# Attention over four batches with two expert layers: values loaded in four parts, and three other pieces of the order moved

## The chip, the cores and the metric

The kernel runs on one core of a Trainium2 chip. The metric is the device time of one execution in microseconds (us). The engines are TensorE (PE; its weight loads are PEld), VectorE (DVE), ScalarE (ACT), GpSimd (POOL) and SyncE (SP), which issues nearly all transfers. L286 is line 286 of the kernel before.

## The reference

Attention with 4 batches, 12 heads, 448 positions and head size 64 mixes the scores over the heads before the softmax (`w_pre`) and the weights after it (`w_post`). Its output, 1792 rows of 768, goes through a layer with a squared ReLU, and then through a layer in which each row goes to one of 8 experts.

```
scores = scale * q @ k.T                              # per batch and head, 448 x 448
scores = einsum('bhij,hg->bgij', scores, w_pre)       # mix the heads
attn   = softmax(scores)
attn   = einsum('bhij,hg->bgij', attn, w_post)        # mix them again
x      = attn @ v                                     # -> 1792 x 768
x      = relu(x @ w_in)**2 @ w_out                    # first layer, d_ff 2048
out    = gate * (relu(x @ w1[e]) @ w2[e]), e = argmax(x @ w_gate)
```

## The kernel before

The order of the instructions on every engine is that in which the code is written; the framework adds the waits and moves nothing.

**Attention** runs in steps. A batch has 45 chunks of 10 query rows by 12 heads (120 partitions); step g belongs to chunk g of all 180, and o = 45 b is the first step of batch b. In step g, `norm` prepares chunk g+1 (sum, reciprocal, and `kp`, the mixing weights `kpost` divided by the sum), `pre` mixes the heads of chunk g+2 on TensorE, takes the maximum on VectorE and the exponential on ScalarE, and `post` multiplies chunk g by its `kp` on TensorE and copies the result out of PSUM into `at`. What else belongs to a step is entered with `on(step, function, ...)`: `scores` (q times k for a tile t of query rows and a head; ScalarE copies the product to `s`, a ring of four buffers, and SP sends it to its place in `t`), `prep` and `load` for the next batch, `pv` (TensorE multiplies `at` of nine chunks, a group `gr`, by the values `v`; half `hf` 0 has heads 0 to 5, half 1 has heads 6 to 11; ScalarE copies the product as `xh`), `pv_lo` (VectorE subtracts `xh` from the product, which gives `xl` and frees the PSUM bank) and `pv_out` (SP writes `xh` and `xl` to memory). A `pv` stands at the end of its step. There is one buffer `vt` for the values of a batch, 1.38 MB.

Before step 0 stands a stretch in which q and k of the first batch are transposed, split into a high and a low part (`zk`, `zl`, `zq`) and scored. There `prep` writes the high part of k twice, once into each half of the partitions; of the two second copies of a pair of heads ScalarE makes one (L211) and GpSimd the other (L209).

**The first layer** (`moe1`) begins inside attention: in the last batch `tail(rel)`, called at the end of step rel of it, runs a plan of weight loads and conversions (rel 27 to 47). In rel 42 to 45 the first products `up` run. The gate of the experts is folded into the weights of the layer: `gate_cols(w, acc, j)` makes two columns of w_out times w_gate on VectorE (L522), and `gate_parts` splits them (L529, L530). For the first two weight tiles, `late[0]` and `late[1]`, this is done late, by `late_gate(i, j)` with j from 0 to 3: the table `late_at` gives the step, and two calls stand in the first visit of `moe1`'s main loop (v = 0). j 0 and 1 need `wga`, j 2 and 3 need `wgb`, which are loaded in rel 39 and 41. The products of v = 0 (`down`, L719) are summed in PSUM banks that the last `pv` used. They do not need the gate's columns; those of v = 1 do.

The lines that the change touches decide on places alone:

```
if b == nb - 1 and c >= LATE:                       # L273, LATE = 32
    nc.scalar.mul(kp, kpost, mx[:, 3:4])
...
first, gap = (0, 1) if b == nb - 1 and gr == NGR - 1 else (1, 1) if b == nb - 1 else (1, 3)
...
if b > 0:
    on(o + 6, load_v, b)
...
late_at = {44: ((0, 0), (0, 1)), 45: ((0, 2), (0, 3)), 46: ((1, 0),), 47: ((1, 1),)}
```

Of the kernel before, what the change touches and what calls it, by code (L numbers as in the profile page):

```python
# [10 lines left out]
F32 = mybir.dt.float32  # L11
# [8 lines left out]
B, H, S, D = 4, 12, 448, 64  # L20
# [4 lines left out]
NP = H // 2  # L25
# [3 lines left out]
TOKT = 112  # L29
# [95 lines left out]
def attention(tc, cst, q, k, v, w_pre, w_post, xscr, nb, tail=None):  # L125
    nc = tc.nc
    GC = 9
    NGR = NCH // GC

    def left(name, bufs=1):  # L130
        return Areas(tc, name, bufs)

    wp, at1, vp, xp, mp = left("wp"), left("at1"), left("vp"), left("xp"), left("mp", 3)
# [10 lines left out]
    vt = {}  # L144
# [4 lines left out]
    halves = (slice(0, 64), slice(64, 128))  # L149

    XB = 4
    LATE = 32

    def load(b, p, nm):

# [20 lines left out]
    def prep(b, p, nm):  # L176

        z = zp.tile([128, 2, S], F32R, tag=f"z{nm}", name=f"z{nm}")
        x = xt.pop((b, p, nm))
        if b == 0:  # L180

            i = 2 * units.index((p, nm))
            pools = [(post_, pre_, post_, pre_, pv_)[j % 5] for j in (i, i + 1)]
            pys = [pool.tile([64, 4, 128], F32, name=pool.name) for pool in pools]
            for o in range(2):
                for r in range(4):
                    nc.tensor.transpose(pys[o][:, r, :TOKT], x[:, o, D * r:D * r + D], ident)
        else:
            py = qk.tile([128, 4, 128], F32, tag="qk", name="py")
            for r in range(4):  # L190
                nc.tensor.transpose(py[:, r, :TOKT], x[:, r].rearrange("p o d -> p (o d)"), ident)
            pys = [py[halves[o]] for o in range(2)]


        def rows(a, o=None):
            a = a if o is None else a[:, o]
            if nm == "k":
                return a.rearrange("q (r t) -> q r t", r=4)
            return a.rearrange("q (t r) -> q t r", r=4)

        yv = [y[:, :, :TOKT] for y in pys]
        if nm == "q":
            yv = [y.rearrange("q r t -> q t r") for y in yv]
        for o in range(2):
            nc.scalar.copy(rows(z[halves[o]], o), yv[o])
        if nm == "k":
            for o in range(2):
                if b == 0 and o and p < NP - 1:
                    nc.gpsimd.tensor_copy(z[halves[0], o], z[halves[1], o].bitcast(F32))  # L209
                elif b == 0:  # L210
                    nc.scalar.copy(rows(z[halves[1 - o]], o), yv[o])  # L211
        yield
        lo = None
        if nm == "k":
            fresh = len(zp.tags.get("zl", (0, ()))[1]) == 0 or zp.tags["zl"][0] < zp.bufs
            lo = zp.tile([128, 2, S], F32R, tag="zl", name="zl")
            if fresh:
                for o in range(2):
                    nc.gpsimd.memset(lo[halves[1 - o], o].bitcast(F32), 0.0)
        zt[b, p, nm] = (z, lo)  # L220
        for o in range(2):
            r = halves[o]
            dst = rows(z[halves[1 - o]], o) if nm == "q" else rows(lo[r], o)
            nc.vector.tensor_sub(dst, yv[o], rows(z[r], o).bitcast(F32))  # L224
            if nm == "k" and b > 0:
                nc.sync.dma_start(out=z[halves[1 - o], o].bitcast(F32), in_=z[r, o].bitcast(F32))
        yield

    def load_v(b):
        vt[b] = vp.tile([TOKT, H, 4, D], F32, name="v")  # L230
        for o in (0, H // 2):
            nc.sync.dma_start(
                out=vt[b][:, o:o + H // 2].rearrange("p h r d -> p h (r d)"),
                in_=v[b, o:o + H // 2].rearrange("h (p r) d -> p h (r d)", r=4),
            )

    tt = {}

# [29 lines left out]
    def norm(b, c):  # L268
        e, mx = st[b, c]
        nc.vector.tensor_scalar_add(mx[:, 2:3], mx[:, 1:2], 1e-9)  # L270
        nc.vector.reciprocal(mx[:, 3:4], mx[:, 2:3])  # L271
        kp = mp.tile([KP, KP], F32, tag="kp", name="kp")
        if b == nb - 1 and c >= LATE:  # L273
            nc.scalar.mul(kp, kpost, mx[:, 3:4])  # L274
        else:
            nc.gpsimd.tensor_scalar_mul(kp, kpost, mx[:, 3:4])  # L276
        st[b, c] = [e, kp]

    at = {}
# [91 lines left out]
    for i, w in enumerate((w_pre, w_post)):  # L371
        nc.sync.dma_start(
            out=wraw[:, i, :],
            in_=w.rearrange("(o h) g -> o h g", o=1).to_broadcast([II, H, H]),
# [14 lines left out]
    kpre, kpost = (wp.tile([KP, KP], F32, name=nm) for nm in ("kpre", "kpost"))  # L389
    mask = cst[:KP, C_MASK:C_MASK + II]  # L390
    for i, kf in enumerate((kpre, kpost)):
        nc.gpsimd.tensor_tensor(
            out=kf.rearrange("p (i g) -> p g i", i=II) if i == 0 else kf.rearrange("p (g i) -> p g i", i=II),
# [2 lines left out]
            op=ALU.mult,  # L396
        )
    nc.gpsimd.tensor_scalar_mul(kpre, kpre, 1.0 / float(D) ** 0.5)
    load_v(0)

    chunks = [(b, c) for b in range(nb) for c in range(NCH)]
    at_step = {}

    def on(g, f, *a):

        rank = 0 if f is go else 2 if f is begin else 1
        at_step.setdefault(g, []).append((rank, f, a))
# [10 lines left out]
    def spread(g, steps, f, *a):  # L418
        on(g, begin, (f, a), f, *a)
        for i in range(1, steps):  # L420
            on(g + i, go, (f, a))
# [5 lines left out]
    for b in range(nb):  # L427
        o = b * NCH
        for h in range(H):
            if b == 0:  # L430
                on(-4 + 8 * h // 12, scores, 0, 1, h)
            on(o + (4 if b == 0 else 2) + 10 * h // 12, scores, b, 2, h)
            on(o + 12 + 10 * h // 12, scores, b, 3, h)
            if b + 1 < nb:
                on(o + 26 + 11 * h // 12, scores, b + 1, 0, h)
                on(o + 37 + 10 * h // 12, scores, b + 1, 1, h)
        for gr in range(NGR):
            end = o + GC * gr + GC
            first, gap = (0, 1) if b == nb - 1 and gr == NGR - 1 else (1, 1) if b == nb - 1 else (1, 3)
            for hf in range(2):  # L440
                for i, f in enumerate((pv, pv_lo)):
                    on(end + first + gap * hf + i, f, b, gr, hf)
            on(end + first + gap + 2, pv_out, b, gr)
        if b + 1 < nb:
            for i, u in enumerate(units):
                spread(o + PREP[i], 2, prep, b + 1, *u)
                on(o + (PREP[i - XB] + 1 if i >= XB else 8 + i), load, b + 1, *u)
        if b > 0:
            on(o + 6, load_v, b)

    n = len(chunks)
    last = max(list(at_step) + [n])
# [28 lines left out]
def moe1(tc, cst, w_in, w_out, w_gate, xscr, tasks, st):  # L481
# [4 lines left out]
    nc = tc.nc  # L486
# [31 lines left out]
    def gate_cols(w, acc, i):  # L518

        dump = wr.tile([128, DM], F32, name="dump")  # L520
        for e in (2 * i, 2 * i + 1):
            nc.vector.scalar_tensor_tensor(  # L522
                out=dump, in0=w, scalar=1.0, in1=wg[e // 4][:, e % 4], op0=ALU.mult, op1=ALU.mult,
                accum_out=acc[:, e:e + 1],
            )
# [135 lines left out]
    }  # L661
    first = [up(0, 0, f) for f in range(GF)]
    UPS = {42: 0, 43: 0, 44: 1, 45: 1}
    late_at = {44: ((0, 0), (0, 1)), 45: ((0, 2), (0, 3)), 46: ((1, 0),), 47: ((1, 1),)}

    def late_gate(i, j):
        f, w, a = late[i]
        gate_cols(w, a, j)
        if j == 3:
            gate_parts(f, a)  # L670
# [86 lines left out]
    for v, (gi, b) in enumerate(order):  # L757

        def do(point):
            for f in tasks.get((v, point), ()):  # L760
                f()

        def conv(ago, stage, kinds="io"):
            i = piece.get(v - ago)
            if i is not None and pieces[i][1] in kinds:
                adv(i, stage)

        f0, f1 = gi * GF, gi * GF + 1
        conv(1, "hi")
        conv(0, "mask", "o")  # L770
        if 0 < v < len(order) - 1 and order[v + 1][1] != b:
            load_x(order[v + 1][1])
        if v > 0:
            for _ in up(gi, b, f0):
                pass
        do(1)
        conv(1, "lo")
        conv(0, "w0", "o")
        if v > 0:
            for i, _ in enumerate(up(gi, b, f1)):  # L780
                if i == 0:
                    do(2)
        conv(0, "w1", "o")
        conv(0, "mask", "i")
        if v in piece:
            load(piece[v] + 2)
        do(3)
        down(gi, b, f0, range(1))
        down(gi, b, f0, range(1, 3))
        do(4)  # L790
        if v == 0:
            late_gate(1, 2)
        down(gi, b, f1, range(1))
        do(5)
        down(gi, b, f1, range(1, 3))
        if v == 0:
            late_gate(1, 3)
        if v == 1:
            first_logits()
        do(6)  # L800
        if (gi, b) == (NG - 1, 2):
            close(y012, wgb, wga)
        do(7)
# [545 lines left out]
```

## Time and profile before

| | |
|---|---|
| median of 3 runs | 1351.9 us (1350.28 to 1353.49) |
| the profiled execution | 1351.87 us, span 1349.7 us |
| busy share of the span | PE 96%, PEld 85%, DVE 72%, ACT 56%, POOL 11% |
| mean granted clock of TensorE | 0.986 |
| attention and the first layer's start | 0 to about 552 us |

The span runs from the first to the last instruction of the profiled execution. The granted clock is 1.00 at 2.4 GHz and 0.50 at 1.2 GHz. Rows of the timeline begin with the start and the duration in us; a bracket at the end gives the idle time of the engine just before and what ended it.

### The profile page before, as it was taken

The numbers are of one execution on the slowest core, as the hardware profiler recorded it, in microseconds if no ns is written. First come the engines' busy times: TensorE is split into PE (matmuls) and PEld (weight loads), VectorE is DVE, ScalarE is ACT, GpSimd is POOL, SyncE is SP. The second block draws the span as 40 slices with busy tenths as digits, with TensorE's granted clock in tenths as the row PEclk, the third lists the DMA queues.
The fourth block names the chain that finished last, engine by engine and source line by source line (L and its number), as shares of the span: only waits on it lengthen the run. The fifth ranks groups of instructions, "written<-read, shape, count | busy, mean of one in ns | idle before, by whom it ended". The sixth has DMA issues, their size and how long they took to land. (4 is left out here: it accounts for less than half of the span.)

```text
span 1349.7 us, 24947 instructions
## 1 busy us (share of the span) xinstructions
PE 1291.3 (96%) x8875; PEld 1146.1 (85%) x8875; DVE 977.3 (72%) x1960; ACT 749.5 (56%) x1479; POOL 149.4 (11%) x229
## 2 busy tenths in 40 slices
PE   6999989998999898899999999999998999999997
PEld 4777867786787767899999999999997899999997
DVE  5567547665766357577895998689648588898887
ACT  6566546654655566353342433334234688889887
POOL 2222211221222110000000000000000111111101
PEclk9999989998999899899999999999999999999999
DMA  7666586548745458546373664636484594556551
GB/s 186 169 161 129 131 158 151 128 118 167 159 122 129 133 114 322 178 189 256 119 277 145 226 264 164 252 123 261 172 297 149 169 377 140 181 176 249 160 187 40
DMA packets 157638, 243.80 MB, mean 181 GB/s; under 512 B 84195, under 2 KB 128579, under 8 KB 149828
## 3 DMA queue, kind: packets, MB, share of 16 engines
q1 hardware_dynamic: 154708, 229.54, 55.3%
q0 software_dynamic: 2800, 12.61, 2.7%
q8 instruction: 72, 1.18, 0.4%
q14 instruction: 58, 0.48, 0.1%
HBM read 236.48 MB, written 23.21 MB: 192 GB/s over the span
## 5 line engine op out<-in xcount | busy, mean ns | idle before, releaser
L265 ACT ACTIVATE mp_e<-pre_pre,mp_mx 120x448 f32<-120x448 f32 x180 | 114.2, 635 | 145.0 <-DVE mp_mx L263 144.2
L286 PEld LDWEIGHTS post_post<-mp_kp,mp_e 120*112 120x112 f32 x1440 | 170.5, 176 | 23.5 <-ACT mp_kp L274 9.0
L286 PE MATMUL post_post<-mp_kp,mp_e 120*112 120x120 f32 x1440 | 178.6, 267 | 3.4 <-ACT mp_kp L274 3.2
L263 DVE TENSOR_REDUCE mp_mx<-pre_pre 120x1 f32<-120x448 f32 x180 | 110.0, 611 | 91.1 <-PE pre_pre L261 90.5
L627 PE MATMUL hp_h<-m1x_xl,m1w_ih 128*128 128x384 f32 (+1 forms) x480 | 155.7, 324 | 2.5 <-DMA m1x_xl<-xscrl 2.4
L636 ACT ACTIVATE m1g_r<-hp_h 128x384 f32<-128x384 f32 (+1 forms) x80 | 37.7, 471 | 214.9 <-PE hp_h L627 204.8
L627 PE MATMUL hp_h<-m1x_xh,m1w_ih 128*128 128x384 f32 (+1 forms) x480 | 156.1, 325 | 0.1
L627 PE MATMUL hp_h<-m1x_xh,m1w_il 128*128 128x384 f32 (+1 forms) x480 | 155.4, 324 | 0.0
L1102 DVE TENSOR_TENSOR m2w_w2l<-m2r_r,m2w_w2h 128x768 fp32r<-128x768 f32 x130 | 116.3, 953 | 33.8 <-ACT m2w_w2h L1101 33.7
L276 POOL TENSOR_SCALAR mp_kp<-wp_kpost,mp_mx 120x120 f32<-120x120 f32 x167 | 97.5, 584 | 371.1 <-DVE mp_mx L271 185.2
L245 PE MATMUL qk_qk<-zp_zk,zp_zq 128*120 128x448 f32 (+1 forms) x192 | 121.0, 630 | 5.9 <-DVE zp_zq L224 1.8
L294 DVE COPY at_at<-post_post 112x480 f32<-112x480 f32 x130 | 85.3, 657 | 50.6 <-PE post_post L286 50.1
L249 ACT COPY sp_s<-qk_qk 120x448 f32<-120x448 f32 (+1 forms) x188 | 96.0, 525 | 38.1 <-DMA tb_t<-sp_s 15.3
L719 PE MATMUL acc_a<-m1w_oh,m1g_gl 128*128 128x384 f32 (+1 forms) x436 | 113.1, 341 | 3.4 <-DVE m1g_gl L639 3.4
L719 PE MATMUL acc_a<-m1w_ol,m1g_gh 128*128 128x384 f32 (+1 forms) x436 | 112.3, 339 | 0.0
L719 PE MATMUL acc_a<-m1w_oh,m1g_gh 128*128 128x384 f32 (+1 forms) x436 | 112.1, 338 | 0.0
L733 DVE TENSOR_TENSOR y_y<-acc_a,y_y 128x384 f32<-128x384 f32 x196 | 96.4, 554 | 11.0 <-PE acc_a L719 10.7
L307 PE MATMUL pv_pv<-at_at,vp_v 112*64 112x90 f32 x1872 | 86.5, 252 | 13.8 <-DMA vp_v<-in_v 12.8
L1101 ACT CAST m2w_w2h<-m2r_r 128x768 fp32r<-128x768 f32 x130 | 99.1, 841 | 0.3 <-PE m2p_a L1163 0.2
L639 DVE TENSOR_TENSOR m1g_gl<-m1g_r,m1g_gh 128x384 fp32r<-128x384 f32 (+1 forms) x78 | 41.2, 528 | 77.7 <-ACT m1g_gh L638 77.7
L307 PEld LDWEIGHTS pv_pv<-at_at,vp_v 112*64 112x64 f32 x1872 | 79.3, 144 | 18.9 <-DMA vp_v<-in_v 13.4
L627 PEld LDWEIGHTS hp_h<-m1x_xl,m1w_ih 128*128 128x128 f32 x480 | 90.1, 188 | 3.3 <-DMA m1x_xl<-xscrl 3.3
(239 smaller groups left out, 2740.4 us busy)
## 6 DMA issues: line engine op xcount, KB each, us to landing
m2r_r<-in_moe_w SPq DMA_DIRECT2D x107, 512.0 KB
m2r_r<-in_moe_w SPq DMA_DIRECT2D x136, 384.0 KB
m1x_xh<-xscrh SPq DMA_DIRECT2D x29, 1152.0 KB
m1x_xl<-xscrl SPq DMA_DIRECT2D x29, 1152.0 KB
m1raw_rawi<-in_moe_w_in SPq DMA_DIRECT2D x16, 768.0 KB
m1raw_rawo<-in_moe_w_out SPq DMA_DIRECT2D x16, 768.0 KB
tb_t<-sp_s SPq DMA_DIRECT2D x48, 210.0 KB
ta_t<-sp_s SPq DMA_DIRECT2D x48, 210.0 KB
```

Of the source, the lines that this page charges most:

```text
L245: nc.tensor.matmul(pq[:m, :S], zq[:, n0:n0 + m], zkh, start=True, stop=False)
L249: eng(s[:m], pq[:m, :S])
L263: nc.vector.tensor_reduce(out=mx[:, 0:1], in_=pm[:KP, :S], axis=AX.X, op=ALU.max, negate=True)
L265: nc.scalar.activation(out=e, in_=pm[:KP, :S], func=AF.Exp, bias=mx[:, 0:1], accum_out=mx[:, 1:2])
L276: nc.gpsimd.tensor_scalar_mul(kp, kpost, mx[:, 3:4])
L286: nc.tensor.matmul(po[:, r].rearrange("p g i -> p (g i)"), ev[:, r], kp, start=True, stop=True)
L307: nc.tensor.matmul(px[64 * o:64 * o + 64, p], vt[b][:, g, r], a[:, r, g].rearrange("p c i -> p (c i)"), start=(r == 0), stop=(r == 3),)
L627: nc.tensor.matmul(ph, w[:, k], x, start=(kt == 0 and i == 0), stop=(kt == KT - 1 and i == 2))
L719: nc.tensor.matmul(p, g[:, c], w[:, HM * h:HM * h + (m if h else HM)], start=(j == 0 and i == 0), stop=(j == GF - 1 and i == 2),)
L733: nc.vector.tensor_add(y, p, y)
L1101: nc.scalar.copy(wh, raw)
L1102: nc.vector.tensor_sub(wl, raw, wh.bitcast(F32))
```

## The change

- `load_v` loads three heads at a time instead of six, so four parts instead of two, at steps o+3, o+5, o+7 and o+9 instead of both at o+6. For the first batch the parts stand at steps 1, 3, 5 and 7 instead of ahead of all steps.
- `pv` of the first four groups of batches 0 to 2 stands at the second and fourth step after its group's end instead of the first and fourth; that of their last group at the first and second instead of the first and fourth, so `pv_out` of it comes two steps earlier. The last batch keeps its places.
- GpSimd scales `kp` for the last 13 chunks too (before: ScalarE).
- In the stretch before step 0 GpSimd makes both second copies of k's high part for pairs 0 to 4 (before: one each).
- Of `late_gate`, (0, 1) goes from rel 44 to 45, (0, 2) and (0, 3) from 45 to 47, (1, 0) from 46 to 47, and (1, 1) from 47 to v = 0.

```
-                if b == 0 and o and p < NP - 1:
-                    nc.gpsimd.tensor_copy(z[halves[0], o], z[halves[1], o].bitcast(F32))
+                if b == 0 and p < NP - 1:
+                    nc.gpsimd.tensor_copy(z[halves[1 - o], o], z[halves[o], o].bitcast(F32))
...
-    def load_v(b):
-        vt[b] = vp.tile([TOKT, H, 4, D], F32, name="v")
-        for o in (0, H // 2):
-            nc.sync.dma_start(
-                out=vt[b][:, o:o + H // 2].rearrange("p h r d -> p h (r d)"),
-                in_=v[b, o:o + H // 2].rearrange("h (p r) d -> p h (r d)", r=4),
-            )
+    def load_v(b, i):
+
+        if i == 0:
+            vt[b] = vp.tile([TOKT, H, 4, D], F32, name="v")
+        o = slice(3 * i, 3 * i + 3)
+        nc.sync.dma_start(
+            out=vt[b][:, o].rearrange("p h r d -> p h (r d)"),
+            in_=v[b, o].rearrange("h (p r) d -> p h (r d)", r=4),
+        )
...
-        if b == nb - 1 and c >= LATE:
-            nc.scalar.mul(kp, kpost, mx[:, 3:4])
-        else:
-            nc.gpsimd.tensor_scalar_mul(kp, kpost, mx[:, 3:4])
+        nc.gpsimd.tensor_scalar_mul(kp, kpost, mx[:, 3:4])
...
-    load_v(0)
...
-            first, gap = (0, 1) if b == nb - 1 and gr == NGR - 1 else (1, 1) if b == nb - 1 else (1, 3)
+            first, gap = (2, 2) if gr < NGR - 1 and b < nb - 1 else (1, 1)
+            if b == nb - 1 and gr == NGR - 1:
+                first = 0
...
-        if b > 0:
-            on(o + 6, load_v, b)
+        for i in range(4):
+            on(o + 3 + 2 * i - 2 * (b == 0), load_v, b, i)
...
-    late_at = {44: ((0, 0), (0, 1)), 45: ((0, 2), (0, 3)), 46: ((1, 0),), 47: ((1, 1),)}
+    late_at = {44: ((0, 0),), 45: ((0, 1),), 47: ((0, 2), (0, 3), (1, 0))}
...
         if v == 0:
+            late_gate(1, 1)
             late_gate(1, 2)
```

On SP, at the start of the second batch, the order before was this (`tb_t` is where scores go, `vp_v` the values, `xscr` the output of `pv_out`, `ld_x` the next batch's q and k):

```order
L338 DMA xscrh_58<-xp_xh_663 768x1x64
L338 DMA xscrl_63<-xp_xl_664 768x1x64
L254 DMA tb_t_237<-sp_s_233 10x12x448
L232 DMA vp_v_404<-in_v 112x6x256 x2
L254 DMA tb_t_237<-sp_s_234 10x12x448
L254 DMA tb_t_237<-sp_s_235 10x12x448
L254 DMA tb_t_237<-sp_s_232 10x12x448
L166 DMA ld_x_593<-in_q 112x8x64
```

In the changed kernel the first part stands ahead of the output of `pv_out`, and a part follows after every three or four other transfers:

```order
L233 DMA vp_v_477<-in_v 112x3x256
L336 DMA xscrh_57<-xp_xh_681 768x1x9
L336 DMA xscrl_62<-xp_xl_682 768x1x9
...
L255 DMA tb_t_237<-sp_s_235 10x12x448
L255 DMA tb_t_237<-sp_s_232 10x12x448
L233 DMA vp_v_477<-in_v 112x3x256
L255 DMA tb_t_237<-sp_s_233 10x12x448
L255 DMA tb_t_237<-sp_s_234 10x12x448
L255 DMA tb_t_237<-sp_s_235 10x12x448
L233 DMA vp_v_477<-in_v 112x3x256
```

So the values no longer follow `pv_out` in one block.

On VectorE, at the end of attention, the order before was this (L639 is the low part of an `up` product, L522 the gate's columns, L323 is `pv_lo` of the last group, half 0 out of `pv_pv` and half 1 out of `pre_pre`):

```order
L639 TENSOR_TENSOR m1w_ol_4451<-m1g_r_4642,m1w_oh_4447 128x384
L522 SCALAR_TENSOR_TENSOR m1raw_dump_4661,m1raw_wog_4442<-m1raw_t_4387,wgb_wgb_4595 128x768 x4
L529 CAST m1w_oh_4444<-m1raw_wog_4442 128x8
L530 TENSOR_TENSOR m1w_ol_4448<-m1raw_wog_4442,m1w_oh_4444 128x8
L323 TENSOR_TENSOR xp_xl_664<-pv_pv_141,xp_xh_663 128x270
L522 SCALAR_TENSOR_TENSOR m1raw_dump_4661,m1raw_wog_4443<-m1raw_t_4333,wga_wga_4563 128x768 x2
L323 TENSOR_TENSOR xp_xl_664<-pre_pre_161,xp_xh_663 128x270
L522 SCALAR_TENSOR_TENSOR m1raw_dump_4661,m1raw_wog_4443<-m1raw_t_4333,wga_wga_4563 128x768 x2
```

In the changed kernel it is this, from the same operation on:

```order
L637 TENSOR_TENSOR m1w_ol_4459<-m1g_r_4650,m1w_oh_4455 128x384
L520 SCALAR_TENSOR_TENSOR m1raw_dump_4669,m1raw_wog_4450<-m1raw_t_4395,wga_wga_4571 128x768 x2
L321 TENSOR_TENSOR xp_xl_682<-pv_pv_141,xp_xh_681 128x270
L321 TENSOR_TENSOR xp_xl_682<-pre_pre_161,xp_xh_681 128x270
L520 SCALAR_TENSOR_TENSOR m1raw_dump_4669,m1raw_wog_4450<-m1raw_t_4395,wgb_wgb_4603 128x768 x4
L527 CAST m1w_oh_4452<-m1raw_wog_4450 128x8
L528 TENSOR_TENSOR m1w_ol_4456<-m1raw_wog_4450,m1w_oh_4452 128x8
L520 SCALAR_TENSOR_TENSOR m1raw_dump_4669,m1raw_wog_4451<-m1raw_t_4341,wga_wga_4571 128x768 x4
```

Two of the gate's operations stand between that L639 and the first `pv_lo` instead of four and their split, and none stands between the two `pv_lo`; all the others come behind them.

## Rows read from the trace of the kernel before

**Rows 1.** The waits of TensorE: us in total, times, longest.
```profile
PE pv_pv L307 <- DMA vp_v<-in_v: 12.8, 3, 4.7
PE acc_a L719 <- DVE xp_xl L323: 6.2, 2, 4.4
PE pre_pre L261 <- DMA ta_t<-sp_s: 5.8, 1, 5.8
...
PE post_post L286 <- ACT mp_kp L274: 3.2, 5, 1.2
```

**Rows 2.** The timeline of TensorE, `pv` of each later batch's first group.
```profile
188.31 3.87 PE L307 MATMUL pv_pv<-at_at,vp_v 112*64 112x90 f32 x48 [4.74 <-DMA vp_v<-in_v]
...
199.88 2.08 PE L307 MATMUL pv_pv<-at_at,vp_v 112*64 112x90 f32 x48
...
315.33 3.87 PE L307 MATMUL pv_pv<-at_at,vp_v 112*64 112x90 f32 x48 [4.03 <-DMA vp_v<-in_v]
...
442.04 3.87 PE L307 MATMUL pv_pv<-at_at,vp_v 112*64 112x90 f32 x48 [4.04 <-DMA vp_v<-in_v]
```

**Rows 3.** Stretches: us; busy of PE, PEld, DVE, ACT, POOL; clock; DMA share, GB/s.
```profile
35.00:40.00 5.00, 4.78 (x13) 2.69 (x12) 1.57 (x4) 1.44 (x4) 0.58 (x1) 0.73 0.75 200
...
190.00:195.00 5.00, 5.00 (x39) 3.82 (x36) 0.97 (x2) 1.11 (x3) 0.00 (x0) 0.53 0.80 189
...
320.00:325.00 5.00, 5.00 (x29) 3.73 (x27) 2.68 (x7) 2.76 (x9) 0.58 (x1) 0.90 0.79 192
...
445.00:450.00 5.00, 5.00 (x59) 3.89 (x58) 1.85 (x5) 1.96 (x5) 0.02 (x1) 0.77 0.37 123
...
545.00:550.00 5.00, 5.00 (x18) 5.00 (x18) 4.83 (x11) 0.00 (x0) 0.00 (x0) 0.53 0.89 158
```

**Rows 4.** The timeline of SP: the issues of the values, first and second batch.
```profile
28.23 1.19 SPq L232 DMA_DIRECT2D vp_v<-in_v  x2
...
179.85 2.52 SPq L232 DMA_DIRECT2D vp_v<-in_v  x2
```

**Rows 5.** The timeline of ScalarE: a copy of scores beside the values' transfer.
```profile
192.51 0.53 ACT L249 COPY sp_s<-qk_qk 120x448 f32<-120x448 f32 x1 [5.88 <-DMA tb_t<-sp_s]
```

**Rows 6.** DMA queues from 168 to 196 us: packets, MB, share of 16 engines.
```profile
q1 hardware_dynamic: 8809, 4.24, 81.3%
```

**Rows 7.** The timeline of TensorE: the first `pre`.
```profile
33.82 1.82 PE L261 MATMUL pre_pre<-tb_t,wp_kpre 120*120 120x448 f32 x2 [5.85 <-DMA ta_t<-sp_s]
```

**Rows 8.** The timeline of ScalarE: scores of head 9 (tile 0) and head 1 (tile 1).
```profile
25.16 0.52 ACT L249 COPY sp_s<-qk_qk 120x448 f32<-120x448 f32 x1
...
29.34 0.53 ACT L249 COPY sp_s<-qk_qk 120x448 f32<-120x448 f32 x1 [0.69 <-DMA tb_t<-sp_s]
```

**Rows 9.** The timeline of VectorE: scores of head 11, tile 0.
```profile
26.62 0.62 DVE L249 COPY sp_s<-qk_qk 120x448 f32<-120x448 f32 x1 [0.62 <-PE qk_qk L246]
```

**Rows 10.** The page's costliest groups: GpSimd's scaling (busy, mean ns, idle before it).
```profile
L276 POOL TENSOR_SCALAR mp_kp<-wp_kpost,mp_mx 120x120 f32<-120x120 f32 x167 | 97.5, 584 | 371.1 <-DVE mp_mx L271 185.2
```

**Rows 11.** The timeline of VectorE in the last steps: a reciprocal, a weight conversion.
```profile
501.65 0.16 DVE L271 RECIPROCAL mp_mx<-mp_mx 120x1 f32<-120x1 f32 x1
...
502.25 0.95 DVE L576 TENSOR_TENSOR m1w_il<-m1raw_t,m1w_ih 128x768 fp32r<-128x768 f32 x1
```

**Rows 12.** The timeline of TensorE: the first layer's first sums.
```profile
542.41 0.45 PE L719 MATMUL acc_a<-m1w_oh,m1w_oh 128*128 128x384 f32 x1 [4.38 <-DVE xp_xl L323]
544.64 0.69 PE L719 MATMUL acc_a<-m1w_oh,m1w_oh 128*128 128x384 f32 x1 [1.78 <-DVE xp_xl L323]
```

**Rows 13.** The timeline of VectorE around them.
```profile
536.43 0.56 DVE L639 TENSOR_TENSOR m1w_ol<-m1g_r,m1w_oh 128x384 fp32r<-128x384 f32 x1 [1.68 <-ACT m1w_oh L638]
537.63 0.96 DVE L522 SCALAR_TENSOR_TENSOR m1raw_dump<-m1raw_t,wgb_wgb 128x768 f32<-128x768 f32 x1 [0.64 <-DMA wgb_wgb<-in_moe_w_gate]
...
541.92 0.43 DVE L323 TENSOR_TENSOR xp_xl<-pv_pv,xp_xh 128x270 fp32r<-128x270 f32 x1
...
557.10 0.56 DVE L639 TENSOR_TENSOR m1g_gl<-m1g_r,m1g_gh 128x384 fp32r<-128x384 f32 x1 [6.24 <-ACT m1g_gh L638]
```

More of the change, by code (lines that the diff above doesn't have):

```diff
@@ L151, in attention @@
     XB = 4
-    LATE = 32
     def load(b, p, nm):
```

## The prediction

> **What bounds the kernel now.** I read the waits of TensorE first, since it is busy in 96% of the span, more than any other engine. The list is led by the places that the change touches: 12.8 us in three waits of `pv` for the values, 6.2 us in two waits of the first layer's sums for `pv_lo`, 5.8 us in one wait of the first `pre`, and 3.2 us in five waits of `post` for ScalarE's `kp` [rows 1]. Elsewhere in attention TensorE runs without a gap worth naming, so a wait taken away there shortens the span, unless another one takes its place.
>
> The timeline then shows that such a wait costs more than its idle time. In each of the batches 1 to 3 TensorE stands for 4.74, 4.03 and 4.04 us, and the 48 matmuls of the `pv` behind it take 3.87 us where those of a later half take 2.08 [rows 2]. The granted clock explains it: it has fallen to 0.50 (1.2 GHz) during the wait and comes back later. In 190 to 195 us its mean is 0.53, so it was low for 4.7 of these 5 us, to 194.7; in 320 to 325 the mean of 0.90 makes 1.0 us, to 321.0; in 445 to 450 the 0.77 makes 2.3 us, to 447.3 [rows 3]. Work at half clock loses half of its time: (194.7 − 188.31)/2 = 3.2, (321.0 − 315.33)/2 = 2.8 and (447.3 − 442.04)/2 = 2.6 us. The three waits cost 12.8 + 8.6 = 21.4 us.
>
> **Values in four parts (steps 3 to 9).** SP issues both halves at 179.85, and TensorE wants them at 188.31 − 4.74 = 183.57 [rows 2, 4]: 3.7 us for 1.38 MB, beside the output of `pv_out` that SP has just issued. Three steps lie between the two halves of `pv`, which start 11.57 us apart [rows 2]; less the clock's 3.2 us and 2 us for the first half itself, a step is about 2.1 us. In the changed kernel the first two parts leave 8 and 6 steps (17 and 13 us) ahead of the half that reads them, the last two 6 and 4 steps (13 and 8 us); in the last batch, whose `pv` keeps its places, the last part has two steps, some 4 to 5 us. Is there room? From 168 to 196 us the queue kept the 16 DMA engines busy for 81.3% [rows 6], 22.8 us of work, in a stretch that would last 28 − 4.74 − 3.2 = 20.1 us without the stall. So all of it would not fit, but the parts start about 6 us earlier, ahead of this burst. I take the three waits as gone.
>
> What remains is late scores: ScalarE waited up to 5.88 us for a buffer of the ring of four while the values travelled [rows 5], and it is in order, so the exponentials stand behind that. Bounds: nothing and 5.88 us per batch. The transfer that it waited for shared the engines with one block of 1.38 MB, and now with parts of 0.34 MB, so I take 1 us in each of the three batches. Term: 21.4 − 3.0 = **18.4 us**.
>
> **The first batch.** Its values were issued at 28.23, just behind the last scores of tile 0 [rows 4]. Head 9's scores, copied by 25.68, had left their buffer at 29.34, 3.66 us later [rows 8]. Head 11's, copied by 27.24 [rows 9], landed only as the first `pre` started, at 33.82 after 5.85 us of idle time [rows 7], if they are what it waited for: 6.6 us. Without the values beside them they should land at 27.24 + 3.66 = 30.9, which gives 2.9 us. The clock was low until 37.7 (mean 0.73 in 35 to 40 [rows 3]), so the low clock lost (37.7 − 33.82)/2 = 1.9 us; a wait shorter by half may still make it fall, so I take 0.9. The second copies: ScalarE loses five of about 0.52 us (the nearest row is a copy of 448 columns [rows 8]). 2.6 us is the upper bound and nothing the lower; VectorE works alongside with four subtractions and two thirds of a copy per pair, at the 0.62 of a copy [rows 9] 2.9 us against ScalarE's 3.3 before, so it takes over as the bound, and (3.3 − 2.9) × 5 = 2 us is left, of which I take half. Term: 2.9 + 0.9 + 1.0 = **4.8 us**.
>
> **GpSimd scales to the end.** The waits on ScalarE's `kp` are 3.2 us [rows 1], the most that this can give. But the operation lasts 0.584 us on GpSimd [rows 10], and between the weight conversions it is VectorE's reciprocal that comes late: in these steps VectorE goes from the reciprocal at 501.65 through the next maximum straight into a conversion at 502.25 [rows 11]. The rows of before give no step with a GpSimd scaling beside a conversion, so the bounds are a gain of 3.2 and a loss of 13 × 0.584 = 7.6 us, should each scaling hold up VectorE for its whole length. I take 0, between a shorter queue on ScalarE and a longer operation.
>
> The Trainium skill speaks against this edit ("SBUF — State Buffer", section "Who interferes with whom"): a VectorE instruction with two SBUF inputs and a GpSimd instruction that reads SBUF exclude each other for their whole length, and the one that issues first goes first. The conversion at 502.25 has two such inputs. No row of before shows the two at once; by the rule the edit would cost, in an estimate, 13 × (501.81 + 0.584 − 502.25) = 1.9 us, and the whole would come out at 1325.
>
> **The other moved `pv`.** The last group's halves of batches 0 to 2 now stand one step apart, so the second waits for `pv_lo` of the first. A step of 2.1 us holds the copy of `xh` and a subtraction of 0.43 us [rows 13]; the bounds are 0 and 0.5 us for each of the three, and I take **−0.5 us** in all.
>
> **The gate's preparations.** TensorE stands 4.38 and 1.78 us for the two `pv_lo` [rows 12]. VectorE reaches the first at 541.92, because after L639 (536.43 + 0.56 = 536.99) it waits 0.64 us for `wgb` and makes four gate operations and their split [rows 13]; 541.92 − 537.63 = 4.29 us for the four and the split makes some 1.0 us each. Now two stand there: `pv_lo` at 539.0, its bank free at 539.5, against the idle time's start at 542.41 − 4.38 = 538.03. So 1.5 us of the first wait stays, and the second goes, since the second `pv_lo` follows at once: 4.38 + 1.78 − 1.5 = 4.7. The low clock lasted until 549.7 (0.53 in 545 to 550 [rows 3]); (549.7 − 544.64)/2 = 2.5 us comes back, if 1.5 us does not make it fall. What is late next is the gate: VectorE has the same work less 0.64, but two operations more behind L639, so it ends near 552.2 instead of 550.86 (557.10 − 6.24 [rows 13]), and its next task, wanted for v = 1 at 557.10 so far, is wanted 7.2 us earlier, at 549.9. It is up to 2.3 us late; TensorE has other sums to make first, so I take 1.2. Term: 4.7 + 2.5 − 1.2 = **6.0 us**.
>
> **Sum.** 18.4 + 4.8 + 0 − 0.5 + 6.0 = 28.7 us off the profiled execution's own 1351.87 us, which is the median of the runs (1351.9): **1323 us**.
>
> **Rivals.**
> *Late scores take the place of the values.* For it: ScalarE's 5.88 us, and an engine share that is near full. Against it: the parts leave earlier and are a quarter of the size. TensorE then stands for 4 us per batch and loses 2.9 by the clock; the first term falls to 21.4 − 20.7 = 0.7, and the time is 1341. Chance 0.13.
> *VectorE is held up in the last 13 steps*, as a mechanism of this kernel: the scaling starts at the reciprocal's end (501.81) and would keep the conversion of 502.25 until 502.4 or later; up to 7.6 us, 1331. Chance 0.10. This is what the skill's rule above would do.
> *The gate's wait only moves.* TensorE waits in v = 1 for what it no longer waits for in v = 0, since VectorE has no less to do: the last term falls to 0, 1329. For it: VectorE is busy without a gap there. Against it: it had 6.24 us of slack behind. Chance 0.10.
> *Slower.* SP is one queue. If the parts among the scores are held there and land after both halves of the first `pv` of all four batches, eight halves wait as three do now, 8 × 7.1 = 57 us for 21.4, less 10.3 gained elsewhere: 25 us slower, 1377. It decides from 31.7 / 8 = 4.0 us lost per half on. Chance 0.04; the last batch's final part is the one with little room.
>
> **How the numbers follow.** The forecast has 0.63. Its own bounds: with all waits gone, the full clock and 2.6 us on ScalarE about 1314; with 3 us per batch of late scores, 3 us at the start and 2.3 at the end about 1337. The range 1315 to 1339 holds the forecast and the second and third rival; what lies above is most of the first and the fourth. A change of 0.2% (2.7 us) is about what a measurement of this kernel can tell from none. Faster in all cases but the last and a part of the first: 0.94, the same 0.02, slower 0.04.
>
> **What would show it.** `pv` no longer among TensorE's waits for a DMA, and the clock at 1.00 around 170 to 190 us of each batch: first term. The first `pre` near 30 us. The first sums of v = 0 with about 1.5 us of idle time, those of v = 1 with 1. Waits of `post` for GpSimd's `kp` of about 3 us. The forecast is wrong if TensorE gets new waits for copies of scores at a batch's start, or for the last part in the last batch.

## The result: 1340 us, faster than before but 17 us above the forecast

| | before | changed |
|---|---|---|
| median on the same chip | 1351.6 us (4 runs) | 1340.1 us (4 runs, 1337.2 to 1341.3) |
| ratio to before | | 0.9911, 95% interval 0.9889 to 0.9932 |
| ratio in a second comparison | | 0.9902, 0.9879 to 0.9925 (5 runs) |
| span of the profiled execution | 1349.7 us | 1335.4 us, the fastest run (1337.18 us) |

The direction is right, but the time lies above the range of 1315 to 1339. The waits of TensorE after the change, to be set beside [rows 1] (us in total, times, longest):

```profile
PE pre_pre L262 <- ACT mp_e L266: 5.4, 3, 3.0
PE acc_a L718 <- DVE m1g_gl L637: 4.0, 5, 1.0
PE pre_pre L262 <- issue: 4.0, 1, 4.0
PE post_post L284 <- POOL mp_kp L274: 3.7, 4, 1.2
...
PE pv_pv L305 <- DMA vp_v<-in_v: 2.5, 1, 2.5
...
PE acc_a L718 <- DVE xp_xl L321: 1.2, 1, 1.2
```

The values' 12.8 us have become 2.5, the first layer's 6.2 have become 1.2, and the first `pre` waits 4.0 instead of 5.8 ("issue": the profile shows nothing that it waited for). New at the head is `pre`, three times, for ScalarE's exponential. The timeline of TensorE shows the three beside the one wait for values that is left:

```profile
181.19 1.01 PE L262 MATMUL pre_pre<-tm_t,wp_kpre 120*120 120x448 f32 x2 [2.97 <-ACT mp_e L266]
304.81 1.01 PE L262 MATMUL pre_pre<-tb_t,wp_kpre 120*120 120x448 f32 x2 [1.16 <-ACT mp_e L266]
427.05 1.01 PE L262 MATMUL pre_pre<-ta_t,wp_kpre 120*120 120x448 f32 x2 [1.28 <-ACT mp_e L266]
437.00 1.47 PE L305 MATMUL pv_pv<-at_at,vp_v 112*64 112x90 f32 x30 [2.55 <-DMA vp_v<-in_v]
```

Each of the first three stands at the start of a batch. ScalarE's timeline shows why in batch 1:

```profile
174.13 0.52 ACT L250 COPY sp_s<-qk_qk 120x448 f32<-120x448 f32 x1
179.98 0.53 ACT L250 COPY sp_s<-qk_qk 120x448 f32<-120x448 f32 x1 [5.32 <-DMA tb_t<-sp_s]
180.41 0.64 ACT L266 ACTIVATE mp_e<-pre_pre,mp_mx 120x448 f32<-120x448 f32 x1
```

The second copy waits 5.32 us for a buffer of the ring of four, that is, for scores copied earlier to reach `t`. The exponential stands behind it on the same engine, and TensorE behind that. SP's timeline shows what stood ahead of those scores:

```profile
167.48 0.44 SPq L233 DMA_DIRECT2D vp_v<-in_v  x1
167.97 0.57 SPq L336 DMA_DIRECT2D xscrh<-xp_xh  x1
168.64 0.67 SPq L336 DMA_DIRECT2D xscrl<-xp_xl  x1
169.36 0.89 SPq L336 DMA_DIRECT2D xscrh<-xp_xh  x1
170.29 1.30 SPq L336 DMA_DIRECT2D xscrl<-xp_xl  x1
171.64 0.66 SPq L336 DMA_DIRECT2D xscrh<-xp_xh  x1
172.34 0.66 SPq L336 DMA_DIRECT2D xscrl<-xp_xl  x1
173.10 1.76 SPq L255 DMA_DIRECT2D tb_t<-sp_s  x2
174.96 0.43 SPq L233 DMA_DIRECT2D vp_v<-in_v  x1
```

These are the six transfers of `pv_out` of the group before, 5 us of issuing. The three stretches that follow (columns as in [rows 3]) show a full set of DMA engines that moves little, then the clock:

```profile
171.00:176.00 5.00, 5.00 (x35) 4.09 (x34) 3.24 (x9) 2.29 (x6) 1.69 (x3) 1.00 1.12 86
176.00:181.00 5.00, 2.22 (x15) 1.60 (x13) 0.66 (x1) 1.02 (x3) 0.06 (x1) 1.00 0.83 201
181.00:186.00 5.00, 4.81 (x16) 3.37 (x17) 3.23 (x11) 3.03 (x9) 1.59 (x3) 0.66 0.83 220
```

From 171 to 176 us the share is 1.12 at 86 GB/s (a share above 1 says that the times of the packets, added up, exceed the time of the 16 engines); TensorE stands in the second row (2.22 us busy of 5), and in the third its clock has fallen, to a mean of 0.66.

**Where the 14.3 us of span came from.** Three marks cut the execution into stretches: the start of the reciprocal of chunk 45 (VectorE L272; the first chunk of batch 1), of the first ReLU of `up` (ScalarE L634) and of the fifth. In the changed kernel they are these rows:

```profile
152.05 0.16 DVE L272 RECIPROCAL mp_mx<-mp_mx 120x1 f32<-120x1 f32 x1
518.37 0.49 ACT L634 ACTIVATE m1g_r<-hp_h 128x384 f32<-128x384 f32 x1 [0.39 <-PE hp_h L625]
553.57 0.49 ACT L634 ACTIVATE m1g_r<-hp_h 128x384 f32<-128x384 f32 x1 [3.00 <-PE hp_h L625]
```

The same marks in before stand at 155.41, 528.65 and 570.25. So batch 0 gained 3.4 us, batches 1 to 3 gained 6.9 (373.24 to 366.32 us), the first products 6.4 (41.60 to 35.19), and the rest gave 2.4 back, 1.4 of it near 961 us, where the clock fell at a wait for `m1x_xl` at which it did not fall in before.

### The profile page after: what moved, and what is told of

It reads as the page before. It is cut to its first block, busy times and chain, and to the rows that moved or that the text cites. A ratio compares the mean times of both kernels' runs of the same rounds, so it can differ in the third digit from the quotient of the medians.

```text
span 1335.4 us, 24980 instructions
## 1 busy us (share of the span) xinstructions
PE 1286.3 (96%) x8875; PEld 1140.2 (85%) x8875; DVE 977.6 (73%) x1960; ACT 743.3 (56%) x1461; POOL 161.1 (12%) x247
## 5 line engine op out<-in xcount | busy, mean ns | idle before, releaser
L284 PEld LDWEIGHTS post_post<-mp_kp,mp_e 120*112 120x112 f32 x1440 | 171.1, 177 | 24.4 <-POOL mp_kp L274 13.8
L634 ACT ACTIVATE m1g_r<-hp_h 128x384 f32<-128x384 f32 (+1 forms) x80 | 37.6, 470 | 218.3 <-PE hp_h L625 205.3
L274 POOL TENSOR_SCALAR mp_kp<-wp_kpost,mp_mx 120x120 f32<-120x120 f32 x180 | 105.2, 584 | 389.5 <-DVE mp_mx L272 209.8
L625 PEld LDWEIGHTS hp_h<-m1x_xh,m1w_ih 128*128 128x128 f32 x480 | 90.6, 189 | 0.3 <-DMA m1x_xh<-xscrh 0.2
L625 PEld LDWEIGHTS hp_h<-m1x_xh,m1w_il 128*128 128x128 f32 x480 | 90.5, 189 | 0.0
```

The source lines that it names most:

```text
L284: nc.tensor.matmul(po[:, r].rearrange("p g i -> p (g i)"), ev[:, r], kp, start=True, stop=True)
L625: nc.tensor.matmul(ph, w[:, k], x, start=(kt == 0 and i == 0), stop=(kt == KT - 1 and i == 2))
```

## Experiments

Theory A: the output of `pv_out` ahead of the scores makes the new stalls, and made the old ones. Theory B: the values' own parts do. All kernels start from the changed one unless said; "the first item" is the first of the change, the values in four parts. The table has the distances between the marks in each kernel's profile in us (rounded after the subtraction) and its ratio to the kernel before on the same chip. Each stretch is that of one profile; the ratios are of the medians. out_late_again is the kernel of out_late once more. The rows are ordered by the middle stretch, on which the two theories differ.

| kernel | to chunk 45 | chunk 45 to first `up` | first to fifth `up` | ratio, 95% interval |
|---|---|---|---|---|
| before | 155.41 | 373.24 | 41.60 | 1 |
| old_values | 153.05 | 371.40 | 35.24 | 0.9943 (0.9920 to 0.9965) |
| ring6 | 151.04 | 369.82 | 35.19 | 0.9911 (0.9878 to 0.9945) |
| changed | 152.05 | 366.32 | 35.19 | 0.9911 (0.9889 to 0.9932) |
| out_o6 | 152.52 | 366.23 | 35.20 | 0.9924 (0.9901 to 0.9947) |
| out_pool | 154.07 | 365.86 | 35.24 | 0.9914 (0.9887 to 0.9942) |
| v0_kp | 153.75 | 364.38 | 35.23 | 0.9897 (0.9875 to 0.9919) |
| after_again (changed) | 151.26 | 363.20 | 35.21 | 0.9902 (0.9879 to 0.9925) |
| out_big | 152.49 | 360.14 | 35.22 | 0.9864 (0.9844 to 0.9884) |
| last_22 | 150.86 | 360.03 | 35.21 | 0.9884 (0.9859 to 0.9909) |
| copies_gate | 153.12 | 359.20 | 41.60 | 0.9924 (0.9900 to 0.9949) |
| out_late | 150.96 | 356.79 | 35.21 | 0.9861 (0.9827 to 0.9896) |
| out_late_again | 151.56 | 356.15 | 35.21 | 0.9842 (0.9825 to 0.9859) |
| before_out | 154.45 | 355.86 | 41.25 | 0.9891 (0.9871 to 0.9911) |
| old_out_late | 153.68 | 355.73 | 35.24 | 0.9835 (0.9816 to 0.9853) |
| novals | 152.78 | 354.15 | 35.19 | not comparable |

**novals.** No values for batches 1 to 3 (`pv` reads those of batch 0).

```
-            on(o + 3 + 2 * i - 2 * (b == 0), load_v, b, i)
+            if b == 0:
+                on(o + 1 + 2 * i, load_v, b, i)
```

> The changed kernel without the loads of the values in batches 1 to 3 (pv reads those of batch 0, so this part of the work is left out). Theory A, the output of pv_out delays the scores: without any values on the queue the first batch step's wait of pre for ScalarE's exponential (2.97 us at 181 in the changed kernel, 1.16 at 305, 1.28 at 427) stays at 2 us or more in batch 1; only the wait of pv in the last batch goes (2.55 us and 1.7 by the clock), so about 4 us less than the changed kernel's 1340, 1336. Theory B, the values' own parts delay the scores: all of these waits go, 5.4 + 1.7 + 4.3, about 11 us less, 1329.

All stalls are gone, also those of `pre`, and the longest wait of ScalarE's copy at the start of batch 1 is a short one for TensorE:

```profile
177.73 0.53 ACT L250 COPY sp_s<-qk_qk 120x448 f32<-120x448 f32 x1 [2.34 <-PE pre_pre L262]
```

So theory A, as put, falls: with `pv_out` in its place but no values beside it, the scores are in time, though SP spends 4.6 us on the six issues (168.17 to 172.81 us) and 5.1 in the changed kernel. The stretch of 354.15 us is the shortest of all. The time of the whole, 1343.7 us, says nothing: other values send other rows to the experts.

**ring6.** `left("sp", 4)` becomes `left("sp", 6)`.

> The changed kernel with six instead of four buffers for the copies of scores. If it is the ring that stops ScalarE (both theories A and B), its waits of 3.5 to 5.3 us for a transfer at a batch's start shrink by the two copies that may go ahead, pre no longer waits for the exponential there, and 5.4 us of idle time and 1.7 of low clock come back: 1340 - 7 = 1333. If instead the scores themselves land too late for pre, the wait only changes its name and the time stays at 1340.

The time stayed at the changed kernel's ratio, as in the second case, but not for the reason given there. `pre` waits no longer for the exponential, and `pv` waits for the values:

```profile
192.35 2.66 PE L305 MATMUL pv_pv<-at_at,vp_v 112*64 112x90 f32 x30 [3.68 <-DMA vp_v<-in_v]
317.57 2.43 PE L305 MATMUL pv_pv<-at_at,vp_v 112*64 112x90 f32 x30 [1.80 <-DMA vp_v<-in_v]
439.79 1.82 PE L305 MATMUL pv_pv<-at_at,vp_v 112*64 112x90 f32 x30 [2.62 <-DMA vp_v<-in_v]
```

With room for more scores ahead of them, the values came late. In this run the number of buffers only decided who waited for the backlog.

**out_late.** `pv_out` moved behind the scores of tile 2.

```
-... vp, xp, mp = ... left("vp"), left("xp"), left("mp", 3)
+... vp, xp, mp = ... left("vp"), left("xp", 2), left("mp", 3)
-            on(end + first + gap + 2, pv_out, b, gr)
+            on(end + first + gap + (2 if gr < NGR - 1 or b == nb - 1 else 12), pv_out, b, gr)
```

> The changed kernel with pv_out of the last group of batches 0 to 2 ten steps later, behind the scores of tile 2, and two buffers for xh and xl so that it can wait. Theory A (pv_out's issues and small packets delay the scores): the waits of pre at 181, 305 and 427 us go, 5.4 us and 1.7 of clock, 1333, and the copy of scores at a batch's start waits under 1 us. Theory B (the values' parts do it): the copy still waits 3 us or more and the time stays near 1340.

The three waits of `pre` and that of `pv` are gone: 1326.1 us, ratio 0.9861 and, repeated, 0.9842. So taking away `pv_out` clears a batch's start as taking away the values does; each is needed for the stall there, and `pv_out` is the one that can move.

It takes a smaller stall along. In the last batch it now stands beside the output of that batch's first group (o+13), and six transfers go out ahead of scores again, now with no values beside them. The timelines of SP, of ScalarE and of TensorE:

```profile
437.87 0.66 SPq L336 DMA_DIRECT2D xscrl<-xp_xl  x1
438.63 13.57 SPq L255 DMA_DIRECT2D tb_t<-sp_s  x8
```

```profile
444.38 0.53 ACT L250 COPY sp_s<-qk_qk 90x448 f32<-90x448 f32 x1 [3.18 <-DMA tb_t<-sp_s]
```

```profile
445.52 1.05 PE L284 MATMUL post_post<-mp_kp,mp_e 120*112 120x120 f32 x8 [1.58 <-ACT at_at L292]
```

This wait of `post` is 1.2 to 1.9 us in the five profiles with the late `pv_out`, and is in none of the other kernels.

**last_22.** `(2, 2) if gr < NGR - 1 and b < nb - 1 or gr == 0` in the line of `first, gap`.

> The changed kernel with the two halves of pv of the last batch's first group at the second and fourth step behind its end (they stood at the first and second), so the last part of the values has four steps instead of two. The wait of pv for the values, 2.55 us at 437, and the low clock behind it, 1.7 us, go: 1340 - 4 = 1336. If the values only land later still, or the later pv holds up the next group, the time stays at 1340 or rises by up to 2.

The wait at 437 us is gone, as expected, but in batch 1 `pv` now waits 1.37 us for the values. The ratio is 0.0027 (3.6 us) below the changed kernel's first and 0.0018 below its second; the intervals overlap, so the gain is not clear of noise. The waits of `pre` stay, 2.9 us in three.

**old_values.** Values and `pv` as before, the rest as changed.

> The changed kernel with the first item of the change undone for batches 1 to 3: the values in two halves at o+6 and pv where it stood before; all else as changed. It measures that item. By the traces' marks the item was worth about 8 us, so a ratio to the kernel before of 0.997 (the changed kernel has 0.9911). If the prediction's first term of 18.4 were right and something else had eaten the gain, the ratio would be 0.9911 + 18.4/1351.9 = 1.005.

`pv` waits for the values almost as long as before:

```profile
PE pv_pv L305 <- DMA vp_v<-in_v: 10.5, 3, 4.0
```

The first item is worth 0.0032 by the first ratio of the changed kernel and 0.0041 by the second, 4 to 6 us; the intervals overlap. By the middle stretch it is 9: 372.3 on average for the two profiles in the old order, 363.3 for four in the changed one (changed, after_again, v0_kp, copies_gate). Both are far below the forecast's 18.4 (17.9 with the other moved `pv`, which this run undoes too).

**before_out.** The kernel before, and the edit of out_late alone.

> The kernel before, with pv_out of the last group of batches 0 to 2 at o+14 instead of o+6 (two buffers for xh and xl), and nothing else. If pv_out is what makes the values late (they are issued right behind it), the three waits of pv for the values shrink from 12.8 us to under 5 and 10 to 15 us come off, ratio 0.990, as much as the four parts brought. If the values are late by their own size in two halves, the waits stay near 12.8 us, ratio 1.000.

The ratio of 0.9891 is 14.7 us, at least as much as the whole change brought (0.9911 and 0.9902; the intervals overlap). Of the 12.8 us that `pv` waited for the values 0.3 is left, and the two halves of the first group run at full clock where one took 3.87 us in [rows 2]:

```profile
182.53 2.08 PE L307 MATMUL pv_pv<-at_at,vp_v 112*64 112x90 f32 x48
...
191.09 2.08 PE L307 MATMUL pv_pv<-at_at,vp_v 112*64 112x90 f32 x48
```

SP's timeline has the values here at

```profile
175.96 1.00 SPq L232 DMA_DIRECT2D vp_v<-in_v  x2
```

Counted from the mark of chunk 45, SP issues the values of batch 1 at 24.4 us in before (179.85, [rows 4]) and at 21.5 us here, 2.9 us earlier. From their issue to the first `pv` it took 8.5 us in before (to 188.31, [rows 2], a wait that they ended) and takes at most 6.6 here (to 182.53, no wait). So in batch 1 `pv_out` made the values late in two ways: by the time of its issues on SP, 2.9 us, and, as far as nothing else differs there, by its load on the DMA engines, 1.9 us or more.

**old_out_late.** old_values and out_late together.

> The kernel of the run old_values (values in two halves, old places of pv) with pv_out of the last groups of batches 0 to 2 at o+14. The four parts and the later pv are all that it lacks against out_late_again. If they bring something once pv_out is out of the way, it is slower than that run by 3 us or more, ratio 0.988 or above. If pv_out alone made the values late, it is as fast, 0.986 or below: the first item of the change then removed a symptom.

Ratio 0.9835 against out_late_again's 0.9842 beside it, stretch 355.73 against 356.15; `pv` waits 0.3 us for the values. With `pv_out` out of the way, two halves at o+6 are as good as four parts; the first item treated a symptom.

**out_big.** out_late, and in `pv_out`'s old place a copy of the same bytes in long rows (added work).

```
+    def again(b, gr):
+        for dst, src in zip(xscr[2], xo[b, gr]):
+            nc.sync.dma_start(out=dst[:, b], in_=src.bitcast(F32))
```

> The kernel of the run out_late, and where pv_out stood before (o+4) a copy of the same xh and xl, the same 0.53 MB, to a scratch in two transfers of rows of 2160 bytes, instead of six transfers of rows of 36 to 256 bytes. If it is pv_out's many small packets and six issues that held up the scores, this costs under 2 us over out_late, ratio 0.987. If it is the bytes, the waits of pre for the exponential or of pv for the values come back, ratio 0.991 or more.

No wait of `pre` came back at a batch's start and 0.3 us of `pv`'s, and the ratio is that of out_late. (The stretch is 3.5 us longer; 1.7 of it is a fall of the clock at 449 us, behind a wait of `post` of 1.92 us that out_late has too, with 1.58 us and no fall.) The DMA view of equal stretches of 5 us tells the two outputs apart. In out_big, 171 to 176 us (queue: packets, MB, share of 16 engines):

```profile
DMA packets 838, 1.23 MB, mean 246 GB/s; under 512 B 64, under 2 KB 619, under 8 KB 837
q1 hardware_dynamic: 837, 1.22, 84.8%
```

In the changed kernel, 171 to 176 us:

```profile
DMA packets 3411, 0.43 MB, mean 86 GB/s; under 512 B 3403, under 2 KB 3410, under 8 KB 3410
q1 hardware_dynamic: 3410, 0.42, 111.4%
```

In the kernel before, 176 to 181 us:

```profile
q1 hardware_dynamic: 3982, 0.46, 111.2%
```

A third of the bytes takes more of the packets' time. The `pv_out` at the start of batch 1 writes 27, 45 and 192 KB twice, 0.54 MB (0.53 in the expectation), in rows of 36, 60 and 256 bytes. As an estimate, at the price of the last row it takes the 16 engines 0.54 × 5 × 1.112 / 0.46 = 6.5 us, at that of out_big 0.54 × 5 × 0.848 / 1.22 = 1.9. (Both stretches hold other transfers too.) But out_big also has two issues on SP, 0.9 us, for six, so it does not part the packets from the issues.

**out_pool.** `pv_out` of the last groups on GpSimd's queue (`eng = nc.gpsimd ...`).

> The changed kernel with the transfers of pv_out of the last group of batches 0 to 2 issued by GpSimd's queue at the same step, instead of SP's: the same packets at the same time, but SP no longer spends 5 us on six issues ahead of the scores. If SP's order is what delays the scores, the waits of pre at a batch's start go and the ratio is 0.986, as with out_late. If the packets in the DMA engines do it, the waits stay and the ratio is 0.991; a GpSimd that is held by its issues would show as waits of post for kp.

This answers neither. GpSimd is held by the issues, about 0.7 us from each to the next, and its scaling comes late:

```profile
169.69 1.02 POOL L337 DMA_DIRECT2D xscrh<-xp_xh  x1
...
173.46 1.39 POOL L337 DMA_DIRECT2D xscrl<-xp_xl  x1
174.20 1.83 POOL L274 TENSOR_SCALAR mp_kp<-wp_kpost,mp_mx 120x120 f32<-120x120 f32 x2
```

So in batch 1 one stall replaced another. In batches 2 and 3 `pv` waits for the values (1.59 and 2.06 us), though nothing of `pv_out` stands ahead of them on SP. But the packets are not the same, as the expectation took them to be. From 168 to 182 us the DMA view has the whole 0.54 MB on GpSimd's queue in 256 packets:

```profile
q0 software_dynamic: 256, 0.54, 22.6%
```

By the share they took 0.226 × 14 = 3.2 us of the 16 engines. So SP's issues and the short packets both went, and stalls stayed. No run keeps one of the two and takes away the other; the parts of 2.9 and 1.9 us under before_out are what the traces show of them, for batch 1 of before.

**out_o6.** The second half of the last group's `pv` at o+4, so `pv_out` at o+6 as before.

> The changed kernel with the second half of the last group's pv of batches 0 to 2 back at the fourth step, so pv_out of it at o+6 as before; the values stay in four parts. If it is the earlier pv_out that spoils the first item, the stretch from the reciprocal of chunk 45 to that of chunk 150 falls from 286.6 to 293.4 us (profiles of the changed order) to about 283, ratio 0.986. If pv_out's packets cost as much at o+6, ahead of or among the parts, the stretch stays at 286 to 294 us and the ratio at 0.991.

The stretch is 366.2 us: it is not the move from o+6 to o+4. Now `pv` waits (6.9 us in four waits) and `pre` does not.

**after_again.** The changed kernel unaltered, beside out_o6.

> The changed kernel itself on the same chip: ratio 0.991 as first measured, the stretch between the two reciprocals 286 to 294 us, with the waits of pre for the exponential at the start of each batch between 1 and 3 us.

Its waits are shorter and elsewhere: `pre` 1.26 and 0.73 us, `pv` 1.71 and 1.94. One order of this stretch gave 359 to 366 us in four profiles (these two, v0_kp and copies_gate). That a queue without slack turns small shifts into stalls of other lengths is my reading, not shown.

**v0_kp and copies_gate.** Each undoes two pieces of the change, far apart.

> The changed kernel with two pieces undone that act 450 us apart and are read from marks in the trace: the values of the first batch ahead of step 0 again, in four issues (the first pre should start about 2.9 us later if the prediction's price of the landing holds, 0 if the values were not what held it), and ScalarE scales kp in the last 13 chunks again (the prediction says 0 between chunk 150 and the first up; the skill's rule on the shared port would make this version 1.9 us faster there). Ratio about 0.993.

> The changed kernel with two other pieces undone: one of the two second copies of k's high part on ScalarE again (the start should become 1.0 us longer by the prediction, 2.6 at most, nothing if VectorE was the bound), and the gate's preparations at their old places (6.0 us longer between the first up and the fifth by the prediction, 0 if their wait only moves to v = 1). Ratio about 0.996.

The gate is clear: first to fifth `up` 41.60 us against 35.19, 6.4 us, with both waits back:

```profile
525.61 0.69 PE L718 MATMUL acc_a<-m1w_oh,m1w_oh 128*128 128x384 f32 x1 [3.91 <-DVE xp_xl L321]
527.83 0.69 PE L718 MATMUL acc_a<-m1w_oh,m1w_oh 128*128 128x384 f32 x1 [1.54 <-DVE xp_xl L321]
```

ScalarE's scaling changes little: from the reciprocal of chunk 150 to the first `up` 72.75 us with it (72.45 in before), and 72.57 to 72.97 in the eight profiles with GpSimd's and with `pv` and `pv_out` in the last batch where the changed kernel has them. The start stays unresolved: 153.75 us to chunk 45 with the values ahead of step 0, 153.12 with the old copies, but twelve profiles with the changed start lie between 150.86 and 154.07 (mean 152.2; the two in the old order, 155.41 and 154.45). In v0_kp the first `pre` waits for a landing again, 5.19 us for `ta_t`, which fits the mechanism but not its price. The ratio of copies_gate, expected at 0.996, is lower; its middle stretch, 359.20 us, is the shortest of that order.

## Why the prediction was wrong

**Values in four parts: 18.4 us forecast, 4 to 9 measured.** The step that failed is "The transfer that it waited for shared the engines with one block of 1.38 MB, and now with parts of 0.34 MB, so I take 1 us in each of the three batches." The values did leave earlier, and in batches 1 and 2 of the changed kernel's profile no `pv` waits for them. But I put the late scores down to the size of the values, and read the 81.3% of [rows 6] as one lump. It holds 8809 packets for 4.24 MB, under 500 bytes each on average, and what made transfers late in this stretch was `pv_out`, by the time of its issues and, less surely, by the load of its short packets: moving it alone brought 14.7 us (before_out), and with it moved the first item is worth nothing (old_out_late). I had noticed that `pv_out` is issued right ahead of the values and moves by two steps, yet priced its move through `pv_lo` alone, none of its packets. Splitting the values took nothing off the engines' work; the backlog moved to the scores (changed), or back to the values (ring6, out_o6).

What the waits cost was sized a little high: 21.4 − 0.5 = 20.9 us for all of it. Moving `pv_out` takes the middle stretch from 373.2 to 355.7 to 356.8 us, 16.5 to 17.5 with the new wait of `post`, and leaving the values out takes it to 354.15, 19.1.

**The first rival is what happened, at a part of its price.** The late scores took the values' place with 5.4 us of waits instead of 12, and the clock fell behind one of the three. That 1340 lies beside this rival's 1341 is in part luck: it has the stretch of batches 1 to 3 gain 0.7 − 0.5 = 0.2 us where 6.9 were gained, and the start gave 1.4 less than forecast and 2.4 were given back at the end. In the last batch the part with "two steps, some 4 to 5 us" came 2.55 us late, the place that the prediction named as the one with little room.

**The first batch: 4.8 forecast, about 2.7 to 3.4 measured.** The first `pre` starts at 30.15 us, as forecast ("near 30 us"), and the start's clock still falls. How the sum divides into landing and copies the runs do not resolve; the 3.3 us for ScalarE's work per pair has no row behind it.

**GpSimd scales to the end: 0 forecast, 0.5 us or less measured.** The waits of `post` for `kp` went from 3.2 to 3.7 us. The second rival, VectorE held up, did not occur. The timelines of GpSimd and VectorE in the changed kernel show a scaling and a conversion with two inputs at once, each as long as the mean of its kind (584 and about 950 ns):

```profile
491.47 0.58 POOL L274 TENSOR_SCALAR mp_kp<-wp_kpost,mp_mx 120x120 f32<-120x120 f32 x1 [1.21 <-PE post_post L284]
```

```profile
491.72 0.95 DVE L574 TENSOR_TENSOR m1w_il<-m1raw_t,m1w_ih 128x768 fp32r<-128x768 f32 x1
```

By the Trainium skill ("SBUF — State Buffer", section "Who interferes with whom") the second should have waited for the first to end; in these rows it did not, and the estimate of 1.9 us does not show in the time. One of the 13 scalings was longer, 0.93 us at 496.96, beside a conversion with one input. GpSimd's spans in the profile are rough.

**The gate's preparations: 6.0 forecast, 6.4 measured**, with 1.24 us left of the first wait (1.5 forecast) and 0.70 in v = 1 (1.2 forecast):

```profile
529.00 0.78 PE L718 MATMUL acc_a<-m1w_oh,m1w_oh 128*128 128x384 f32 x2 [1.24 <-DVE xp_xl L321]
542.38 0.62 PE L718 MATMUL acc_a<-m1w_oh,m1g_gl 128*128 128x384 f32 x2 [0.70 <-DVE m1g_gl L637]
```

**Not foreseen:** 2.4 us given back after the fifth `up`. The fall of the clock near 961 us stands in 8 of the 15 profiles after before's and not in the others, at waits of about 2.1 us in each; what decides it stays open. So does what makes one order's stalls differ from run to run.

**The range.** Its upper bound of 1337 adds 9, 3 and 2.3 us to a forecast that already holds 3.0 and 1.2 of them; without counting these twice it is 1323.2 + 6 + 3 + 1.1 = 1333.

The best version is the changed kernel with `pv_out` late: 1326 us, ratio 0.984 to 0.986, and as good with the values in two halves. It still has the wait of `post` in the last batch.

## What to carry to other kernels

When a transfer is late, split the queue's share by transfer, packets beside bytes, and ask what stands ahead of it: here 0.54 MB in six issues and rows of 36 to 256 bytes held up 1.38 MB of values behind it. Cutting up the victim handed the wait to the next one on the queue, and a deeper buffer chose who waited (ring6). Moving the transfer that stood ahead cleared the place; look then at what stands behind it at its new one. And check that an experiment changes only what its name says: the same bytes on another queue went in other packets (out_pool).

## What the hardware showed

The price of short rows was unexpected. In before's stretch of 176 to 181 us, 3982 packets of 116 bytes on average have 1.112 × 5 × 16 us / 3982 = 22 ns each in the profile; in out_big 837 packets of 1458 bytes have 81 ns. Per byte that is 3.5 times as much. (In the first stretch the times add up to more than the engines had, so 22 ns is what a packet took there and not the least that it can take.) The Trainium skill ("DMA: Bandwidth & Descriptors", section "Why small descriptors are slow (HBM only)") names a fixed overhead for each packet, 27% at 256 bytes; the rows agree in direction, and no run here has one size of packet alone.
